# A fused memory-attention and squared-ReLU feed-forward kernel: scores copied out of PSUM at once, z pieces kept whole, weights converted two units at a time, and all batches in one pipeline of units

## The chip, the cores and the metric

The kernel runs on one core of one Trainium2 chip. The metric is the device time of one execution in microseconds (us). Three timed runs of the kernel before gave 759.39, 759.55 and 759.56 us, a median of 759.55 us. One more execution was taken with the hardware profiler on; all durations below come from it.

## What is computed

The reference, cut to what matters, with 8 batches (B), 8 heads (H), 512 tokens (S), 32 memory states (Ns) of 64 numbers each (D), a model width of 512 and a hidden width of 2048:

```python
scores = scale * np.matmul(x, state.transpose(0, 1, 3, 2))
scores = scores - scores.max(-1, keepdims=True)
a = np.exp(scores)
a /= a.sum(-1, keepdims=True) + 1e-09
xread = np.matmul(a, state)
scores2 = scale * np.matmul(state, x.transpose(0, 1, 3, 2))
...
sread = np.matmul(a2, x)
attn = np.concatenate([xread, sread], axis=2)
...
h = x @ w_in
r = np.maximum(h, 0.0)
return ((r * r) @ w_out).astype(np.float32)
```

The tokens read from the states (a softmax over 32 states), the states read from the tokens (a softmax over 512 tokens), and the 8 x (512 + 32) rows that come out go through a feed-forward layer with a squared ReLU. The weights arrive as 64-bit floating-point numbers, everything else as 32-bit ones.

## The kernel before, in words

**One unit of work.** The hidden width is cut into 16 slices of 128 (NFC). For one batch and one slice, a *unit* is `up` and `down` in `mlp` (L263 to L313). `up` makes `ph`, 128 hidden numbers by 512 tokens, in 6 matmuls; then a ReLU on ScalarE (`r`, L276), the square (ScalarE for the first 10 units, L278, VectorE for the rest, L280), and the split into a high and a low part (`g_hi` on ScalarE, L81; `g_lo` on VectorE, L82). `down` multiplies these by a slice of `w_out` into four PSUM tiles `po`, 12 matmuls (L300). `down` of a unit comes two `up`s later. Every precise product is done as three: high by high, low by high, high by low. There are 128 units for the tokens, and then 16 narrower ones for all 256 state rows together.

**z instead of xread.** The tokens' rows are never formed. Since xread is a times state, xread @ w_in is a @ (state @ w_in). The kernel makes z = state @ w_in for each batch in *pieces* of 1, 2 or 4 slices (`z_piece`, L110). A piece is 8 small matmuls (L130), each on a part of the array (64 rows by 32 columns), then a split into `z_hi` and `z_lo`.

**Attention.** `scores` makes `pst` (both score matrices at once, L167) in 8 such small matmuls. From `pst`, still in PSUM, VectorE makes a blockwise transposed copy `q1` for the softmax over states (`turn1`, L200), and then takes the maximum over tokens (`exps2`, L182), after which ScalarE reads `pst` again for the exponentials (L185). `soft1` and `soft1b` (L205 to L221) finish the softmax over the states and give `a_hi` and `a_lo`, which `up` needs. `turn` and `read` (L224 to L255) give the states' rows, `sr`. The tiles `pst`, `pz`, `pt` and `pr` all live in one PSUM buffer (`ps_x`, tag "px", one buffer), one after the other.

**Weights.** Each unit's slice of `w_in` and of `w_out` is loaded as 512 KB of doubles into one of 5 buffers (`load_w`, RAW = 5) and turned into singles by one ScalarE and three VectorE instructions (`singles`, L92 to L101). `w_out` is also split, the low part on GpSimd. All of this is done once, within the first 103 us, beside the first units.

**The order of the work.** The program is written as units in a row; between any two halves of a unit `aux` puts in what is due: conversions (`weights`), z pieces (`z_due`) and attention steps (`reads`), each queue by its due times. A scheduler then fixes the order on each engine by the order of writing, and moves an instruction ahead of others where it expects the engine to be idle. Each engine runs its own instructions strictly in that fixed order. The list BOTH sets how the first two batches take turns: batch 0 has units 0 to 7, batch 1 units 0 to 11, batch 0 the rest, batch 1 the rest; the other batches follow whole. Each such stretch is one call of `mlp` and ends with its own last two `down`s. The state rows go through another call at the very end.

## Time and profile before

| | |
|---|---|
| Median of 3 runs | 759.55 us (759.39 to 759.56) |
| The profiled execution's own time | 759.13 us |
| Its span in the profile, first to last instruction | 757.3 us |
| What lies outside the span | 1.83 us |
| TensorE (PE) busy | 687.0 us, 91% of the span |
| VectorE (DVE) busy | 399.4 us, 53% |
| ScalarE (ACT) busy | 282.1 us, 37% |
| GpSimd (POOL) busy | 44.3 us, 6% |
| Mean granted TensorE clock | 0.977 |

How to read it: PE is TensorE's matrix multiplies, PEld its weight loads. A line such as `327.67 0.79 PE L300 MATMUL po<-wo_hi,g_hi ... x1 [2.83 <-ACT g_hi L81]` says that at 327.67 us a matmul of line 300 began and took 0.79 us; before it the engine had been idle for 2.83 us, until ScalarE had written `g_hi` on line 81. Matmuls overlap, so the distance from one start to the next is what one costs. The kernel's small matmuls are shown twice each (16 in the trace for 8 written). "PEclk" is the share of the full clock that TensorE was granted.

### The profile page before, as it was taken

How to read it: one execution, taken by the hardware profiler on the slowest of the kernel's cores; microseconds unless marked ns; L12 is line 12 of the kernel's file. 1: busy time of each engine (PE TensorE's matmuls, PEld its weight loads, DVE VectorE, ACT ScalarE, POOL GpSimd, SP SyncE). 2: the span in 40 equal slices, each digit the busy share in tenths (PEclk: the TensorE clock that was granted, in tenths of full speed). 3: DMA queues.
4: the chain of work that ended last, by engine and by line, in shares of the span. 5: the costliest groups of instructions: out<-in, count | busy, mean ns of one | idle time of the engine just before them, and what ended most of it. 6: DMA issues, size and time to landing. Idle time of an engine off the chain costs nothing.

```text
span 757.3 us, 9704 instructions
## 1 busy us (share of the span) xinstructions
PE 687.0 (91%) x3896; PEld 504.7 (67%) x3896; DVE 399.4 (53%) x624; ACT 282.1 (37%) x479; POOL 44.3 (6%) x31
## 2 busy tenths in 40 slices
PE   1477979999969999989998999899998999999997
PEld 0145657777736777757775768577776776778896
DVE  5999953343566724483346433562447543334543
ACT  3566653232333523352334323242324333323442
POOL 0234310000010100010000100010001000000000
PEclk9999989999979999999999999999999999999999
DMA  9755500000333000310031001300020101000101
GB/s 343 260 167 164 187 1 0 1 3 6 112 111 96 20 1 1 112 57 4 1 112 56 4 0 57 112 1 0 20 92 1 57 0 57 1 0 1 57 1 28
DMA packets 16172, 43.60 MB, mean 58 GB/s; under 512 B 1536, under 2 KB 2560, under 8 KB 15104
## 3 DMA queue, kind: packets, MB, share of 16 engines
q1 hardware_dynamic: 15936, 42.74, 16.1%
q8 instruction: 30, 0.49, 0.3%
q10 hardware_dynamic: 192, 0.26, 0.1%
q14 instruction: 14, 0.11, 0.1%
HBM read 34.08 MB, written 8.91 MB: 57 GB/s over the span
## 4 chain that ended last, share of the span: by engine, by line
PE 77%; DVE 10%; issue 7%; ACT 2%; DMA 2%; POOL 0%; SPq 0%; ACTq 0%; POOLq 0%; DVEq 0%
PE po L300 46%; PE ph L274 23%; PE pz L130 6%; DMA wi_raw<-w_in 2%; DVE wof L97 1%; DVE wi L97 1%; DVE q L200 1%; DVE wi L101 1%; DVE m L207 1%; DVE nm L182 1%; PE pr L244 1%; DVE wof L101 1%; PE pst L167 1%; ACT g_hi L81 1%; PE pt L232 1%
## 5 line engine op out<-in xcount | busy, mean ns | idle before, releaser
L300 PE MATMUL po<-wo_hi,g_hi 128*128 128x512 f32 x544 | 224.3, 412 | 21.7 <-ACT g_hi L81 21.7
L300 PE MATMUL po<-wo_lo,g_hi 128*128 128x512 f32 x544 | 218.7, 402 | 0.0
L280 DVE TENSOR_TENSOR ph<-ph,r 128x512 f32<-128x512 f32 (+1 forms) x134 | 88.8, 666 | 196.6 <-ACT r L276 196.3
L276 ACT ACTIVATE r<-ph 128x512 f32<-128x512 f32 (+1 forms) x144 | 82.6, 575 | 261.8 <-PE ph L274 261.7
L300 PE MATMUL po<-wo_hi,g_lo 128*128 128x512 f32 x544 | 155.9, 396 | 0.0
L300 PEld LDWEIGHTS po<-wo_hi,g_hi 128*128 128x128 f32 x544 | 105.3, 194 | 73.2 <-ACT g_hi L81 37.0
L82 DVE TENSOR_TENSOR g_lo<-ph,g_hi 128x512 fp32r<-128x512 f32 (+1 forms) x144 | 94.9, 660 | 78.3 <-ACT g_hi L81 42.7
L300 PEld LDWEIGHTS po<-wo_lo,g_hi 128*128 128x128 f32 x544 | 105.5, 194 | 21.6
L300 PEld LDWEIGHTS po<-wo_hi,g_lo 128*128 128x128 f32 x544 | 101.4, 189 | 26.2 <-issue 5.0
L81 ACT CAST g_hi<-ph 128x512 fp32r<-128x512 f32 (+1 forms) x144 | 81.1, 564 | 91.2 <-DVE ph L280 63.0
L274 PE MATMUL ph<-a_hi,z_hi 128*128 128x512 f32 x256 | 84.5, 414 | 6.8 <-ACT a_hi L81 3.4
L274 PE MATMUL ph<-a_lo,z_hi 128*128 128x512 f32 x256 | 80.8, 398 | 1.8 <-DVE a_lo L82 1.8
L274 PE MATMUL ph<-a_hi,z_lo 128*128 128x512 f32 x256 | 82.2, 402 | 0.0
L130 PE MATMUL pz<-wi,sp_raw 64*32 64x512 f32 (+2 forms) x592 | 56.1, 583 | 25.6 <-ACT wo_hi L81 9.7
L274 PEld LDWEIGHTS ph<-a_hi,z_hi 128*128 128x128 f32 x256 | 47.0, 193 | 28.9 <-ACT a_hi L81 6.3
L274 PEld LDWEIGHTS ph<-a_hi,z_lo 128*128 128x128 f32 x256 | 49.1, 194 | 15.3 <-issue 4.2
L82 DVE TENSOR_TENSOR z_lo<-pz,z_hi 128x1024 fp32r<-128x1024 f32 (+2 forms) x39 | 39.9, 1028 | 35.8 <-ACT z_hi L81 35.8
L274 PEld LDWEIGHTS ph<-a_lo,z_hi 128*128 128x128 f32 x256 | 48.7, 191 | 13.6 <-DVE a_lo L82 2.5
L81 ACT CAST z_hi<-pz 128x1024 fp32r<-128x1024 f32 (+2 forms) x39 | 33.3, 860 | 39.4 <-PE pz L130 39.4
L82 POOL TENSOR_TENSOR a_lo<-at,a_hi 128x1024 fp32r<-128x1024 f32 x7 | 17.1, 2436 | 469.6 <-ACT a_hi L81 393.4
L130 PEld LDWEIGHTS pz<-wi,sp_raw 64*32 64x32 f32 x592 | 9.3, 110 | 47.4 <-issue 15.7
L82 POOL TENSOR_TENSOR wo_lo<-wof,wo_hi 128x512 fp32r<-128x512 f32 x16 | 22.5, 1406 | 65.6 <-ACT wo_hi L81 65.6
(61 smaller groups left out, 406.9 us busy)
## 6 DMA issues: line engine op xcount, KB each, us to landing
wi_raw<-w_in SPq DMA_DIRECT2D x16, 512.0 KB, 3.7
xt_raw<-xT SPq DMA_DIRECT2D x8, 1024.0 KB, 4.8
wo_raw<-w_out SPq DMA_DIRECT2D x16, 512.0 KB, 4.5
xn_raw<-xn SPq DMA_DIRECT2D x8, 1024.0 KB, 5.6
out<-sum SPq DMA_DIRECT2D x32, 256.0 KB, 2.3
sp_raw<-stP SPq DMA_DIRECT2D x8, 64.0 KB, 1.9
out<-os__5498 SPq DMA_DIRECT2D x2, 64.0 KB, 1.7
out<-os__5498 ACTq DMA_DIRECT2D x2, 64.0 KB, 2.0
```

The source lines that it names most:

```text
L81: nc.scalar.copy(out=hi, in_=src)
L82: eng_lo.tensor_sub(out=lo, in0=src, in1=hi.bitcast(F32))
L97: nc.vector.scalar_tensor_tensor(out=bits, in0=high, scalar=-0x80000000, in1=bits, op0=ALU.bitwise_and, op1=ALU.bitwise_or,)
L101: nc.vector.scalar_tensor_tensor(out=bits, in0=low, scalar=29, in1=bits, op0=ALU.logical_shift_right, op1=ALU.bitwise_or,)
L130: nc.tensor.matmul(pz[g][j * N:(j + 1) * N], lhsT=state[b][rows, j, :], rhs=wi[rows, j, cols], start=True, stop=True,)
L167: nc.tensor.matmul(pst[j * N:(j + 1) * N, g, :], lhsT=state[b][rows, j, :], rhs=my["t"][rows, j, :], start=True, stop=True,)
L182: nc.vector.tensor_reduce(out=nm2, in_=pst, axis=AX.X, op=ALU.max, negate=True)
L200: nc.vector.transpose(out=my["q1"][:, gs].rearrange("p g j n -> p (g j n)"), in_=my["pst"][:, gs].rearrange("p g s -> p (g s)"),)
L274: nc.tensor.matmul(ph, lhsT=w, rhs=v, start=i == 0, stop=i == len(todo) - 1)
L276: nc.scalar.activation(r, ph, AF.Relu)
L280: nc.vector.tensor_mul(out=ph, in0=ph, in1=r)
L300: nc.tensor.matmul(po[t], lhsT=g, rhs=w, start=i == 0 and j == 0, stop=i == last and j == 2)
```

## The change

Nothing changes in what is computed. The edits:

- **z pieces** are written under a raised priority (HURRY), so that the scheduler places a piece's 8 matmuls together and early.
- **Scores**: `scores` now ends with a ScalarE copy of `pst` into `e2`; the maximum and the exponentials of `exps2` read that copy, so `pst` is held only until that copy and `turn1` are done. `exps2` moves behind the other softmax in the order. For batch 0 the scores and the softmax over states are written under raised priority.
- **The states' read**: the eight scalings on VectorE become one multiply and four copies on GpSimd. The low parts of `w_out`, and batch 1's three softmax steps that were on GpSimd, go to VectorE.
- **Conversions** take two units at a time: 1 MB loads into 3 buffers, instructions twice as wide, one `wof` buffer instead of two. The first pair of `w_in` is loaded and converted in halves.
- **One pipeline**: `mlp` takes a list of all parts, the state rows as the last, and runs their units in one loop, so the last two `down`s of a part stand between the next part's `up`s. `r` has one buffer instead of two. The first 16 units square on ScalarE, not the first 10.
- **BOTH** becomes batch 0 units 0 to 3, batch 1 units 0 to 7, batch 0 the rest, batch 1 the rest. The attention of a batch may begin when the batch two before it has ended, so batch 2's may now begin 8 units before its own first unit, where it was 4.

```diff
-    RAW = 5
-    BOTH = ((0, 8), (1, 12), (0, NFC), (1, NFC))
+    RAW = 3
+    BOTH = ((0, 4), (1, 8), (0, NFC), (1, NFC))
...
+    HURRY = 120
...
         def run():
+            with tc.high_priority(offset=HURRY):
+                make()
...
+            nc.scalar.copy(out=my["e2"], in_=pst)
 
         def exps2():
-            pst, nm2 = my["pst"], my["nm2"]
-            nc.vector.tensor_reduce(out=nm2, in_=pst, axis=AX.X, op=ALU.max, negate=True)
+            e2, nm2, s2 = my["e2"], my["nm2"], my["s2"]
+            nc.vector.tensor_reduce(out=nm2, in_=e2, axis=AX.X, op=ALU.max, negate=True)
...
-                pool_for(b == 1).tensor_sub(out=q1, in0=q1, in1=wide(my["m1"]))
+                nc.vector.tensor_sub(out=q1, in0=q1, in1=wide(my["m1"]))
...
-                pool_for(b == 1).tensor_mul(out=q1, in0=q1, in1=wide(my["s1"]))
+                nc.vector.tensor_mul(out=q1, in0=q1, in1=wide(my["s1"]))
...
-                split(pair[0][:, gs], pair[1][:, gs], my["at"][:, gs], pool_for(b > 0))
+                split(pair[0][:, gs], pair[1][:, gs], my["at"][:, gs], (nc.gpsimd if b > 1 else nc.vector))
...
+            rd = sb.tile([P, NG, D], F32, name="rd", bufs=1)
+            nc.vector.tensor_mul(
+                out=rd, in0=pr[:, :, :D], in1=my["s2"].rearrange("p (g o) -> p g o", o=1)
...
-                    nc.vector.tensor_scalar_mul(
-                        sr[b // GB][at:at + N, c:c + D], pr[own, g, :D], my["s2"][own, g:g + 1]
-                    )
+                nc.gpsimd.tensor_copy(
...
-    def mlp(width, fcs, first, rows, aux):
+    def mlp(parts, aux):
...
-            r = sb.tile([P, S], F32, name="r", bufs=2)[:, :width]
+            r = sb.tile([P, S], F32, name="r", bufs=1)[:, :width]
             nc.scalar.activation(r, ph, AF.Relu)
-            if units[0] < 10:
+            if n < NFC:
...
-        for i in range(len(fcs) + 2):
-            if i <= last:
-                up(fcs[i])
+        for n in range(len(todo_) + 2):
+            if n < len(todo_):
+                up(n)
                 aux()
-            if i >= 2:
-                down(i - 2)
-            if i <= last:
+            if n >= 2:
+                down(n - 2)
+            if n < len(todo_):
                 aux()
...
-        raw = sb.tile([P, DM, 2], I32, name=f"{kind}_raw", tag="raw", bufs=RAW)
+        raw = sb.tile([P, 2 * DM, 2], I32, name=f"{kind}_raw", tag="raw", bufs=RAW)
...
-        wf = sb.tile([P, DM], F32, name="wof", bufs=2)
-        singles(wf, raw)
-        split(wo[0][:, fc, :], wo[1][:, fc, :], wf, nc.gpsimd)
+        wf = sb.tile([P, 2, DM], F32, name="wof", bufs=1)
+        singles(wf, raw.rearrange("p (u e) w -> p u e w", u=2))
+        split(wo[0][:, 2 * k:2 * k + 2, :], wo[1][:, 2 * k:2 * k + 2, :], wf, nc.vector)
...
-        return [w["pad"], w["load_t"], w["scores"], p[0], w["exps2"], p[1], p[2]]
+        return [w["pad"], w["load_t"], w["scores"], p[0], p[1], p[2], w["exps2"]]
...
-    mlp(NS, range(NFC), first, rows, lambda: None)
+    mlp([batch(*p) for p in parts] + [states()], aux)
```

What the instructions' fixed order shows of it, at three places. In these rows a name ending in a number is one buffer of that name, "x5" is the count of equal rows, and the line numbers are those of the kernel that the rows are from.

**First place: TensorE, inside a later batch.** The kernel before, where a z piece (`pz`) of 8 small matmuls stands among the large ones of `up` (`ph`) and `down` (`po`):

```order
L300 MATMUL po_2818<-wo_hi,g_lo 128x512
L130 MATMUL pz<-wi,sp_raw 32x512 x5
L274 MATMUL ph<-a_hi,z_hi 128x512 x2
L274 MATMUL ph<-a_hi,z_lo 128x512 x2
L274 MATMUL ph<-a_lo,z_hi 128x512 x2
L130 MATMUL pz<-wi,sp_raw 32x512
L300 MATMUL po_2815<-wo_hi,g_hi 128x512
```

The same engine in the changed kernel, at a piece of a later batch:

```order
L307 MATMUL po_1556<-wo_hi,g_lo 128x512
L132 MATMUL pz<-wi,sp_raw 32x512 x8
L307 MATMUL po_1553<-wo_hi,g_hi 128x512
L307 MATMUL po_1553<-wo_lo,g_hi 128x512
L307 MATMUL po_1554<-wo_hi,g_hi 128x512
```

The pieces that stood in two to four places now stand in one. Over the whole program the 37 pieces stood in 55 groups (2 of 128 columns, 10 of 256, 43 of 512) and now stand in 37 (2, 7 and 28). The scores `pst` go the other way: 8 groups before, 13 after (five of the eight are cut into 6 and 2). `pt` goes from 17 groups to 13, and `pr` from 8 to 13.

**Second place: TensorE, where the scores of batch 4 are made.** The kernel before, with `down` (`po`) finished for every unit whose `up` is done, and two `up`s open at once around the scores `pst`:

```order
L300 MATMUL po_2244<-wo_hi,g_lo 128x512
L274 MATMUL ph<-a_hi,z_hi 128x512 x4
L167 MATMUL pst<-xt_raw,sp_raw 32x512 x8
L274 MATMUL ph<-a_hi,z_lo 128x512 x2
L274 MATMUL ph<-a_lo,z_hi 128x512 x2
L274 MATMUL ph<-a_hi,z_lo 128x512 x2
L274 MATMUL ph<-a_lo,z_hi 128x512 x2
L300 MATMUL po_2241<-wo_hi,g_hi 128x512
```

The changed kernel at the scores of the same batch:

```order
L281 MATMUL ph<-a_lo,z_hi 128x512 x2
L169 MATMUL pst<-xt_raw,sp_raw 32x512 x6
L307 MATMUL po_2126<-wo_hi,g_hi 128x512
L307 MATMUL po_2126<-wo_lo,g_hi 128x512
L307 MATMUL po_2127<-wo_hi,g_hi 128x512
...
L307 MATMUL po_2129<-wo_hi,g_lo 128x512
L169 MATMUL pst<-xt_raw,sp_raw 32x512 x2
L281 MATMUL ph<-a_hi,z_hi 128x512 x2
L281 MATMUL ph<-a_hi,z_lo 128x512 x2
L281 MATMUL ph<-a_lo,z_hi 128x512 x2
L307 MATMUL po_2126<-wo_hi,g_hi 128x512
```

Before, the scores stood when 52 `down`s were done and two `up`s (53 and 54) were in the making; now they begin when 51 `up`s and 48 `down`s are done, so that three units' `down`s are still to come. For batch 2 the scores stood after 32 `up`s, its own first unit being number 33; now they stand after 27.

**Third place: VectorE, behind the eighth `g_lo`.** The kernel before; `wi` and `wof` are the slices of the two weights under conversion, `sum` is the output of the first part:

```order
L82 TENSOR_TENSOR g_lo<-ph,g_hi 128x512
L97 SCALAR_TENSOR_TENSOR wof<-wo_raw,wof 128x512
L101 SCALAR_TENSOR_TENSOR wi<-wi_raw,wi 128x4x128
L101 SCALAR_TENSOR_TENSOR wof<-wo_raw,wof 128x512
L93 TENSOR_SCALAR wof<-wof 128x512
...
L321 COPY sum<-po_324 128x512
L321 COPY sum<-po_326 128x512
...
L82 TENSOR_TENSOR z_lo<-pz,z_hi 128x1024
L82 TENSOR_TENSOR g_lo<-ph,g_hi 128x512 x2
```

The changed kernel from the same `g_lo`:

```order
L79 TENSOR_TENSOR g_lo<-ph,g_hi 128x512
L94 SCALAR_TENSOR_TENSOR wi<-wi_raw,wi 128x4x256
L79 TENSOR_TENSOR g_lo<-ph,g_hi 128x512
L79 TENSOR_TENSOR wo_lo<-wof,wo_hi 128x1024
L98 SCALAR_TENSOR_TENSOR wi<-wi_raw,wi 128x4x256
L90 TENSOR_SCALAR wof<-wof 128x1024
L79 TENSOR_TENSOR g_lo<-ph,g_hi 128x512
L94 SCALAR_TENSOR_TENSOR wof<-wo_raw,wof 128x1024
L98 SCALAR_TENSOR_TENSOR wof<-wo_raw,wof 128x1024
L79 TENSOR_TENSOR g_lo<-ph,g_hi 128x512
```

Before, 15 instructions, 12 of them conversions, stood between the eighth `g_lo` and the ninth. Now there is one, and then at most four up to the next.

More of the change, by code (lines that the diff above doesn't have):

```diff
@@ L284, in up, with down @@
             split(hi, lo, ph, nc.vector)
-            gs[fc] = hi, lo
-        def down(i):
-            fc = fcs[i]
-            hi, lo = gs.pop(fc)
+            gs[n] = hi, lo
+        def down(n):
+            p, i = todo_[n]
+            nt, last, po = p["width"] // P, len(p["fcs"]) - 1, p["po"]
+            hi, lo = gs.pop(n)
             if not po:
@@ L429, in memory_attention_then_relu2_ffn @@
         while i <= fcs[-1]:
-            new = at[i] == now + i - fcs[0]
             n = ZC
-            if new:
+            if at[i] == now + i - fcs[0]:
                 n = 1 if i < 2 else 2
-            cover = range(i, i + n)
-            pieces.append((now + i - fcs[0], b, cover))
+            pieces.append((now + i - fcs[0], b, range(i, i + n)))
             i += n
@@ L441, in z_due @@
             first, b, cover = pieces[0]
-            if slot[0] < 2 * (first - 2) or ("wi", cover[-1]) in queue[converted[0]:]:
+            if slot[0] < 2 * (first - 3) or cover[-1] not in ready:
                 break
@@ L448, in memory_attention_then_relu2_ffn @@
     for s_ in (
-        w["pad"], load_next, w["load_t"], *[load_next] * (RAW - 1), convert_next, z_due,
-        w["scores"], p[0], p[1], q[0], q[1], p[2], q[2], w["exps2"], convert_next, z_due,
+        w["pad"], load_next, w["load_t"], load_next, load_next, convert("wi", 0, early), z_due,
     ):
         emit(s_)
+    with tc.high_priority():
+        for s_ in (w["scores"], p[0], q[0], p[1], q[1], p[2], q[2]):
+            emit(s_)
+    for s_ in (convert("wi", 0, late), z_due, w["exps2"]):
+        emit(s_)
     weights, reads = Ahead(), Ahead()
-    for m in range(NFC):
-        weights.add([convert_next] * (2 if m + 2 < NFC else 1), 2 * at[m])
+    for k in range(NK):
+        steps = [convert("wi", k + 1)] if k + 1 < NK else []
+        weights.add(steps + [convert("wo", k)], 2 * at[2 * k])
     for b in range(1, B + LATE):
@@ L471, in memory_attention_then_relu2_ffn, with batch, first @@
     sums = {}
-    for b, fcs in parts:
-        while any(w[2] not in emitted for w in attentions[b][2]):
-            reads.next()
-        def first(fc, b=b):
+    def batch(b, fcs):
+        def first(fc):
+            while any(w[2] not in emitted for w in attentions[b][2]):
+                reads.next()
             c, i = divmod(fc, ZC)
@@ L497, in rows @@
                 )
-        mlp(S, fcs, first, rows, aux)
-    while reads.done < len(reads.steps):
-        reads.next()
-    NS = B * N
-    x2_hi = sb.tile([P, NCC, NS], F32R, name="x2_hi", tag="a_hi", bufs=2)
-    x2_lo = sb.tile([P, NCC, NS], F32R, name="x2_lo", tag="a_lo", bufs=2)
-    for i in range(NGB):
-        pt = ps_x.tile([P, NCC, P], F32, name="pt2", tag="px")
-        for cc in range(NCC):
-            nc.tensor.transpose(
-                out=pt[:, cc, :], in_=sr[i][:, cc * P:(cc + 1) * P], identity=ident
-            )
-        split(x2_hi[:, :, i * P:(i + 1) * P], x2_lo[:, :, i * P:(i + 1) * P], pt, nc.vector)
@@ L533, in memory_attention_then_relu2_ffn, with states, turn2, run @@
-    mlp(NS, range(NFC), first, rows, lambda: None)
+        return dict(width=S, fcs=fcs, first=first, rows=rows)
+    def states():
+        NS = B * N
+        x2 = []
+        def turn2(i):
+            def run():
+                if not x2:
+                    x2.extend(
+                        sb.tile([P, NCC, NS], F32R, name=n, tag=t, bufs=2)
+                        for n, t in (("x2_hi", "a_hi"), ("x2_lo", "a_lo"))
+                    )
+                own = slice(i * P, (i + 1) * P)
+                pt = ps_x.tile([P, NCC, P], F32, name="pt2", tag="px")
+                for cc in range(NCC):
+                    nc.tensor.transpose(
+                        out=pt[:, cc, :], in_=sr[i][:, cc * P:(cc + 1) * P], identity=ident
+                    )
+                split(x2[0][:, :, own], x2[1][:, :, own], pt, nc.vector)
+            return run
+        def first(fc):
+            while reads.done < len(reads.steps):
+                reads.next()
+            w_hi = sb.tile([P, NCC, P], F32R, name="wi_hi", tag="z_hi", bufs=2)
+            w_lo = sb.tile([P, NCC, P], F32R, name="wi_lo", tag="z_lo", bufs=2)
+            split(w_hi, w_lo, wi[:, :, fc * P:(fc + 1) * P], nc.vector)
+            return [
+                (w[:, cc, :], v[:, cc, :])
+                for w, v in ((w_hi, x2[0]), (w_lo, x2[0]), (w_hi, x2[1]))
+                for cc in range(NCC)
+            ]
+        def rows(t, po):
+            tile_ = sb.tile([P, DM], F32, name="os_", tag="raw", bufs=RAW)
+            move(t, tile_, po)
+            for i in range(GB):
+                at = (t * GB + i) * R + S
+                queue = nc.scalar if i % 2 else nc.sync
+                queue.dma_start(out=out[at:at + N, :], in_=tile_[i * N:(i + 1) * N, :])
+        reads.add([turn2(i) for i in range(NGB)], 2 * ends[B - 1] - 2, 2 * ends[B - 1] - 8)
+        return dict(width=NS, fcs=range(NFC), first=first, rows=rows)
```

122 lines of the change are left out of this document (61 added, 61 removed).

## The prediction

> **What bounds the kernel now.** I read the stretches of time first, then TensorE's waits, then the timelines around each wait. Each stretch gives its length, the busy time of PE, PEld, DVE, ACT and POOL, the granted clock, the DMA engines' share and GB/s:
>
> ```profile
> 0.00:25.00 25.00, 4.18 (x64) 1.14 (x64) 17.36 (x35) 10.93 (x22) 1.98 (x7) 1.00 0.90 333
> 25.00:50.00 25.00, 13.25 (x54) 7.10 (x55) 25.00 (x42) 13.61 (x25) 7.46 (x5) 1.00 0.61 202
> 50.00:75.00 25.00, 20.15 (x107) 14.26 (x106) 25.00 (x37) 14.92 (x25) 9.70 (x6) 0.99 0.50 167
> 75.00:100.00 25.00, 18.82 (x80) 13.12 (x80) 24.63 (x37) 17.73 (x32) 8.29 (x7) 0.91 0.44 147
> 125.00:150.00 25.00, 25.00 (x118) 18.06 (x118) 9.19 (x13) 7.53 (x12) 0.00 (x0) 1.00 0.00 1
> ```
>
> From 25 to 100 us VectorE is full and TensorE has holes; behind that TensorE is full, with holes at a few places. So in the start an edit is worth what it takes from VectorE or reorders there, and later what it takes from TensorE's own row of matmuls, or from its waits. Those waits from 100 us on (total, times, longest) are:
>
> ```profile
> PE po L300 <- ACT g_hi L81: 19.7, 9, 5.7
> PE pt L232 <- DVE z_lo L82: 4.2, 1, 4.2
> PE pz L130 <- ACT e L185: 2.8, 1, 2.8
> PE pt L232 <- DVE sr L253: 0.4, 1, 0.4
> ```
>
> With one of 0.3 us that a later row shows (at 223.36) they come to 27.4 us, the one that ends at 99.31 us counted with them. Four of the nine in the first row are alike. This is the one at the scores of batch 4, TensorE first, then VectorE:
>
> ```profile
> 324.21 0.62 PE L274 MATMUL ph<-a_lo,z_hi 128*128 128x512 f32 x2
> 327.67 0.79 PE L300 MATMUL po<-wo_hi,g_hi 128*128 128x512 f32 x1 [2.83 <-ACT g_hi L81]
> 331.06 1.09 PE L130 MATMUL pz<-wi,sp_raw 64*32 64x512 f32 x16
> ```
>
> ```profile
> 322.90 1.25 DVE L200 STREAM_TRANSPOSE q<-pst 128x1024 f32<-128x1024 f32 x1 [3.31 <-PE pst L167]
> 324.08 1.19 DVE L182 TENSOR_REDUCE nm<-pst 128x2 f32<-128x1024 f32 x1
> 325.19 1.20 DVE L207 TENSOR_REDUCE m<-q 128x32 f32<-128x1024 f32 x1
> 326.31 0.69 DVE L280 TENSOR_TENSOR ph<-ph,r 128x512 f32<-128x512 f32 x1
> ```
>
> All `down`s are done there, so TensorE has nothing until the two open units are squared, and the squares stand on VectorE behind three instructions on the scores.
>
> **Waits that go: 27.4 us.** In the changed order three units' `down`s are still to come when the scores begin. What six matmuls of `up` and twelve of `down` take, and a ScalarE pass over 1024 columns:
>
> ```profile
> 121.02 1.40 PE ph L274 x6
> 122.41 2.79 PE po L300 x12
> ```
>
> ```profile
> 317.32 1.02 ACT L81 CAST z_hi<-pz 128x1024 fp32r<-128x1024 f32 x1 [3.48 <-PE pz L130]
> ```
>
> Three `down`s are 8.4 us of cover. VectorE needs 3.4 us from the first of its three instructions to the square (322.90 to 326.31), and ScalarE's new copy of the scores adds about 1.0 us ahead of the second. So the four waits of 2.83 us go. The two waits of batch 2 (4.2 and 2.8 us) go since its scores now stand five units ahead of its first `up`. I count the small ones as gone as well, and add 2.5 us for new ones: their number is unknown, between nothing and what the old small ones come to, twice over.
>
> **Slow matmuls behind the waits: 10.3 us.** After a wait TensorE runs at half speed for a while:
>
> ```profile
> 92.53 1.05 PE L130 MATMUL pz<-wi,sp_raw 64*32 64x512 f32 x4
> 99.31 0.79 PE L300 MATMUL po<-wo_hi,g_hi 128*128 128x512 f32 x1 [5.72 <-ACT g_hi L81]
> 103.02 1.11 PE L130 MATMUL pz<-wi,sp_raw 64*32 64x256 f32 x16
> 215.01 1.96 PE L130 MATMUL pz<-wi,sp_raw 64*32 64x512 f32 x16 [2.82 <-ACT e L185]
> 223.36 1.22 PE L274 MATMUL ph<-a_hi,z_hi 128*128 128x512 f32 x2 [0.26 <-ACT a_hi L81]
> ```
>
> Eight `po` matmuls stand between 327.67 and 331.06: 3.39 us where eight warm ones take 8 x 0.23 = 1.85, so 1.5 us lost, four times: 6.0. Between 99.31 and 103.02 it is 1.8. At batch 2 the pieces take 1.96 for 1.09 and 1.22 for 0.62; with the transposes between them taken alike (1.0) that is 2.5. [...]
>
> **z pieces kept whole: 11.5 us.** A whole piece and a quarter of one, as the kernel before has them:
>
> ```profile
> 338.70 1.09 PE L130 MATMUL pz<-wi,sp_raw 64*32 64x512 f32 x16
> 339.72 0.50 PE L300 MATMUL po<-wo_hi,g_hi 128*128 128x512 f32 x1
> 348.23 1.05 PE L130 MATMUL pz<-wi,sp_raw 64*32 64x512 f32 x4
> 349.21 0.50 PE L300 MATMUL po<-wo_hi,g_hi 128*128 128x512 f32 x1
> ```
>
> From start to next start the whole takes 1.02 us and the quarter 0.98: splitting a piece doubles its price. The `po` behind takes 0.1 us longer than its neighbours, so a part costs 1.1. The order loses 15 parts of 512 columns and 3 of 256. One of them (92.53) stood in front of a wait and cost nothing: 14 x 1.1 = 15.4. For the narrow ones I take 0.7, between half and the whole: 2.1. Against that, the scores are cut in two five times: 5 x 1.1 = 5.5. `pt` and `pr` together gain one part, between nothing and 1.1; I take 0.5. Net 11.5. Its ends: 6 if a part costs 0.6, 13 if the scores' cut is free.
>
> **The start: nothing up to the eighth `g_lo`, then the wait of 5.72 us goes (counted above).** VectorE's instructions, their distances, and what GpSimd does to them:
>
> ```profile
> 79.22 1.22 DVE L82 TENSOR_TENSOR z_lo<-pz,z_hi 128x1024 fp32r<-128x1024 f32 x1
> 80.35 0.68 DVE L97 SCALAR_TENSOR_TENSOR wof<-wo_raw,wof 128x512 int32<-128x512 int32 x1
> 82.50 0.42 DVE L93 TENSOR_SCALAR wof<-wof 128x512 int32<-128x512 int32 x1
> 82.83 0.68 DVE L97 SCALAR_TENSOR_TENSOR wi<-wi_raw,wi 128x512 int32<-128x512 int32 x1
> 83.44 0.68 DVE L82 TENSOR_TENSOR g_lo<-ph,g_hi 128x512 fp32r<-128x512 f32 x1
> 87.74 0.68 DVE L82 TENSOR_TENSOR g_lo<-ph,g_hi 128x512 fp32r<-128x512 f32 x1
> 43.63 2.39 DVE L97 SCALAR_TENSOR_TENSOR wof<-wo_raw,wof 128x512 int32<-128x512 int32 x1
> ```
>
> ```profile
> 43.31 2.16 POOL L208 TENSOR_TENSOR q<-q,m 128x1024 f32<-128x1024 f32 x1
> ```
>
> Undisturbed distances are 1.13 us (79.22 to 80.35) for two inputs of 1024, 0.61 for 512, and 0.33 for a conversion's first step. At these, the order of before has 67.7 us of VectorE work up to the end of the eighth `g_lo`, which came at 88.4 (87.74 + 0.68). 7.6 us were idle (25.00 - 17.36 in the first stretch), so 13.1 us are stretching; the last two rows show it, a step of 0.68 us taking 2.39 beside a GpSimd subtraction.
>
> The changed order has 74.5 us up to there: 24 double conversion steps x 1.13, 13 first steps x 0.60 (no row has one at 1024; between 0.33 and 0.67), 6 single steps (3.1), 5 `wo_lo` that were on GpSimd (5.7), 8 `g_lo` (4.8), 19.8 for the two softmaxes, 3.4 of it from GpSimd, and 6.2 for the rest. GpSimd has nothing in this time, so no stretching. Waits come on top, since loads are now 1 MB:
>
> ```profile
> wi_raw<-w_in SPq DMA_DIRECT2D x16, 512.0 KB, 3.7
> xn_raw<-xn SPq DMA_DIRECT2D x8, 1024.0 KB, 5.6
> ```
>
> VectorE's second pair waits for 1 MB behind `xt`: some 2.4 us more idle, 10 in all. Later two loads are issued only as a buffer comes free, 5.6 us and a 1.0 us ScalarE step ahead of their use; ScalarE stands still for them with `r` and `g_hi` queued behind, and TensorE waits for those. Walking the order, I get 3 us there. 74.5 + 10 + 3 = 87.5, against 88.4 before: even. Ends: 81 with no waits, 97 if the last four loads each wait half their length more. Behind it, 12 conversion steps stood before the next `g_lo`; now at most four instructions, under 4.2 us, stand between two. That is what TensorE takes for a unit (1.40 + 2.79), so the wait goes.
>
> The remaining edits I cost at nothing: the states' read and the squares stand beside a TensorE that is full, VectorE being busy 9.19 of 25.00 us there; the narrow units' loop at the end has TensorE full already.
>
> **The sum.** 757.3 - 27.4 - 10.3 - 11.5 + 2.5 = 710.6 us of span. The profiled execution took 759.13, 1.83 outside the span, and the runs' median is 759.55, 0.4 more, which is within what I round: 712.
>
> **The rivals.**
>
> *The scores' waits stay.* VectorE still has two long instructions behind the scores ahead of a square, and ScalarE a copy. For it: the same instructions made the wait before. Against: 8.4 us of `down`s as cover. Price: 4 x (2.83 + 1.5) = 17.3, so 729.
>
> *The stretching is not GpSimd's doing.* Then VectorE, full already, gets 9.1 us of new work (5 `wo_lo`, three softmax steps) and keeps 13.1 us of stretching: the start ends 13 us later, at 725. Against it: 2.39 us beside a GpSimd instruction, 0.68 elsewhere. [...]
>
> *Slower: one `r` for two.* The ReLU of a unit may start only when the square of the one before has read `r`:
>
> ```profile
> L280 DVE TENSOR_TENSOR ph<-ph,r 128x512 f32<-128x512 f32 (+1 forms) x134 | 88.8, 666 | 196.6 <-ACT r L276 196.3
> L276 ACT ACTIVATE r<-ph 128x512 f32<-128x512 f32 (+1 forms) x144 | 82.6, 575 | 261.8 <-PE ph L274 261.7
> ```
>
> If that put half a microsecond into each of the 112 units squared on VectorE, 56 us would come: 768. It decides from (759 - 712) / 112 = 0.42 us a unit. Against: 0.58 + 0.67 us a unit of 4.2, and both engines wait 196 and 262 us for that very chain's input, so there is slack.
>
> **How the numbers follow.** The forecast 0.73, the scores' waits 0.11, the stretching 0.08, `r` 0.04; 0.02 that gains and losses cancel, 0.02 for better than the range. The range 702 to 728 holds the forecast with its ends (start 7 better, or 9 worse with the parts at 0.6) and the stretching rival. Differences up to 0.2% are what a measurement here can't tell from none. Faster 0.94, same 0.02, slower 0.04.
>
> **What would show it.** Right: TensorE's waits behind 100 us sum to a few us; no 2.83 us wait at scores; `pz` in 37 groups; the eighth `g_lo` near 88 us and TensorE without a hole of over 2 us behind it; no conversion step of over 1.3 us. Wrong: waits of `po` on `g_hi` after scores; the full stretch of VectorE reaching past 105 us; ReLUs that wait for VectorE.

## The result, and the profile after

The changed kernel takes **702.85 us** (median of 4 runs, 701.79 to 704.15) where the kernel before takes 759.47 (759.31 to 759.56): a ratio of 0.9255, 95% interval 0.9238 to 0.9273. The forecast was 712, in a range from 702 to 728. The profiled execution of the changed kernel took 703.47 us, with a span of 701.7.

The first row of each page says what kind of time went. Busy time, share of the span and instructions by engine, before:

```profile
PE 687.0 (91%) x3896; PEld 504.7 (67%) x3896; DVE 399.4 (53%) x624; ACT 282.1 (37%) x479; POOL 44.3 (6%) x31
```

and after:

```profile
PE 658.0 (94%) x3896; PEld 495.8 (71%) x3896; DVE 371.2 (53%) x528; ACT 289.2 (41%) x470; POOL 24.3 (3%) x44
```

TensorE runs the same 3896 instructions in 29.0 us less busy time, and it is idle 43.7 us (701.7 - 658.0) where it was idle 70.3 (757.3 - 687.0), 26.6 less. Together that is the whole difference of the spans, 55.6 us. So half of the gain is waiting that went, and half is the same matmuls taking less time.

**Waiting.** The stretches of time after, with the columns as before:

```profile
25.00:50.00 25.00, 14.86 (x79) 7.71 (x80) 25.00 (x36) 15.36 (x24) 0.00 (x0) 1.00 0.62 215
50.00:75.00 25.00, 17.69 (x93) 11.95 (x93) 23.02 (x30) 15.64 (x23) 0.00 (x0) 0.96 0.39 148
75.00:100.00 25.00, 25.00 (x120) 19.94 (x120) 22.85 (x25) 17.63 (x27) 0.00 (x0) 0.97 0.40 147
```

TensorE is full from 75 us on (it was busy for 18.82 of the 25 us from 75 to 100), and the list of waits has no row at all between 95 us and the end. The last wait of the program, from TensorE's timeline, with one ahead of it:

```profile
63.88 0.73 PE L281 MATMUL ph<-a_hi,z_hi 128*128 128x512 f32 x2 [2.36 <-ACT a_hi L78]
...
72.44 0.50 PE L307 MATMUL po<-wo_hi,g_hi 128*128 128x512 f32 x1 [3.25 <-ACT g_hi L78]
...
73.06 0.63 PE L307 MATMUL po<-wo_hi,g_hi 128*128 128x512 f32 x1
```

The scores of batch 4 after, TensorE:

```profile
356.72 1.08 PE L169 MATMUL pst<-xt_raw,sp_raw 64*32 64x512 f32 x12
357.72 0.50 PE L307 MATMUL po<-wo_hi,g_hi 128*128 128x512 f32 x1
...
360.68 1.05 PE L169 MATMUL pst<-xt_raw,sp_raw 64*32 64x512 f32 x4
361.66 0.72 PE L281 MATMUL ph<-a_hi,z_hi 128*128 128x512 f32 x2
...
363.15 0.39 PE L307 MATMUL po<-wo_hi,g_hi 128*128 128x512 f32 x1
...
365.89 0.39 PE L307 MATMUL po<-wo_hi,g_hi 128*128 128x512 f32 x1
```

and VectorE:

```profile
362.82 1.25 DVE L205 STREAM_TRANSPOSE q<-pst 128x1024 f32<-128x1024 f32 x1 [0.95 <-ACT e L181]
363.99 1.18 DVE L185 TENSOR_REDUCE nm<-e 128x2 f32<-128x1024 f32 x1
365.09 0.69 DVE L287 TENSOR_TENSOR ph<-ph,r 128x512 f32<-128x512 f32 x1
```

The square still stands behind two long instructions on the scores. But three `down`s (from 357.72, 363.15 and 365.89) are open when the scores begin, and TensorE is never out of work until the squared unit is ready.

**Busy time.** The small matmuls grouped by shape, with their total busy time and the mean of one in ns, before:

```profile
L130 PE MATMUL pz<-wi,sp_raw 64*32 64x512 f32 x448 | 46.9, 618 | 2.8 <-ACT e L185 2.8
...
L167 PE MATMUL pst<-xt_raw,sp_raw 64*32 64x512 f32 x128 | 10.5, 715 | 4.8 <-DVE z_lo L82 4.8
...
L130 PE MATMUL pz<-wi,sp_raw 64*32 64x256 f32 x112 | 7.8, 492 | 13.4 <-ACT wo_hi L81 9.7 <-ACT e L185 3.6
```

and after:

```profile
L132 PE MATMUL pz<-wi,sp_raw 64*32 64x512 f32 x448 | 31.4, 617 | 5.5 <-DVE z_lo L79 5.5
L169 PE MATMUL pst<-xt_raw,sp_raw 64*32 64x512 f32 x128 | 15.6, 715 | 8.0 <-DVE z_lo L79 5.9 <-DMA xt_raw<-xT 2.1
...
L132 PE MATMUL pz<-wi,sp_raw 64*32 64x256 f32 x112 | 5.1, 422 | 7.2 <-DVE wi L98 7.2
```

The wide z pieces give 15.5 us for 15 parts less, the scores take 5.1 us more for 5 parts more: about 1 us a part in both, with the same number of matmuls. The mean of one matmul (618 and 617 ns) does not show this price, only the total does.

**The start.** The low parts `g_lo` on VectorE, the eighth and ninth:

```profile
87.84 0.68 DVE L79 TENSOR_TENSOR g_lo<-ph,g_hi 128x512 fp32r<-128x512 f32 x1
...
89.57 0.68 DVE L79 TENSOR_TENSOR g_lo<-ph,g_hi 128x512 fp32r<-128x512 f32 x1
```

The eighth ends at 88.5 us, against 88.4 before and 87.5 forecast. The ninth follows after one conversion step, and TensorE does not wait. At 99.31 us before and at 91.40 after, TensorE has ended the same ten `up`s and eight `down`s, so the two traces can be cut there (the changed kernel has one z piece of 256 columns more behind it, 0.6 us). Length, TensorE's busy time, granted clock, before:

```profile
0.00:99.31 99.31, 55.71 (x301) 0.98 0.62 214
99.31:757.30 657.99, 631.26 (x3596) 0.98 0.10 34
```

and after:

```profile
0.00:91.40 91.40, 53.13 (x316) 0.98 0.62 229
91.40:701.70 610.30, 604.88 (x3581) 1.00 0.11 37
```

7.9 us of the gain lie in the start and 47.7 behind it, 26.4 of these in busy time and 21.3 in waits.

### The profile page after: what moved, and what is told of

It is laid out like the page before. It is cut to its first block, busy times and chain, and to the rows that moved or that the text cites. A ratio compares the mean times of both kernels' runs of the same rounds, so it can differ in the third digit from the quotient of the medians.

```text
span 701.7 us, 9604 instructions
## 1 busy us (share of the span) xinstructions
PE 658.0 (94%) x3896; PEld 495.8 (71%) x3896; DVE 371.2 (53%) x528; ACT 289.2 (41%) x470; POOL 24.3 (3%) x44
## 4 chain that ended last, share of the span: by engine, by line
PE 89%; DVE 7%; DMA 1%; issue 1%; ACT 1%; SPq 0%
PE po L307 53%; PE ph L281 28%; PE pz L132 4%; PE pst L169 2%; DMA wi_raw<-w_in 1%; PE pr L246 1%; PE pt L234 1%; DVE wi L94 1%; DVE wi L98 1%; DVE wof L94 1%; DVE wof L98 1%; DVE wo_lo L79 0%; DVE wi L90 0%; DVE z_lo L79 0%; DVE m L212 0%
## 5 line engine op out<-in xcount | busy, mean ns | idle before, releaser
L307 PE MATMUL po<-wo_hi,g_hi 128*128 128x512 f32 x544 | 217.5, 400 | 4.4 <-ACT g_hi L78 4.4
L307 PE MATMUL po<-wo_lo,g_hi 128*128 128x512 f32 x544 | 214.8, 395 | 0.0
L287 DVE TENSOR_TENSOR ph<-ph,r 128x512 f32<-128x512 f32 (+1 forms) x128 | 84.9, 663 | 149.6 <-ACT r L283 149.6
L78 ACT CAST g_hi<-ph 128x512 fp32r<-128x512 f32 (+1 forms) x144 | 81.2, 564 | 131.2 <-DVE ph L287 89.0
L307 PEld LDWEIGHTS po<-wo_hi,g_hi 128*128 128x128 f32 x544 | 102.4, 188 | 38.3 <-ACT g_hi L78 7.7
L307 PEld LDWEIGHTS po<-wo_lo,g_hi 128*128 128x128 f32 x544 | 102.7, 189 | 25.2 <-issue 4.2
L281 PE MATMUL ph<-a_hi,z_hi 128*128 128x512 f32 x256 | 84.3, 409 | 4.4 <-ACT a_hi L78 2.8
L281 PE MATMUL ph<-a_hi,z_lo 128*128 128x512 f32 x256 | 81.9, 398 | 0.0
L281 PE MATMUL ph<-a_lo,z_hi 128*128 128x512 f32 x256 | 79.5, 393 | 1.0 <-DVE a_lo L79 1.0
L281 PEld LDWEIGHTS ph<-a_hi,z_hi 128*128 128x128 f32 x256 | 46.9, 191 | 30.0 <-issue 7.5
L281 PEld LDWEIGHTS ph<-a_hi,z_lo 128*128 128x128 f32 x256 | 48.7, 190 | 14.8 <-issue 4.2
L281 PEld LDWEIGHTS ph<-a_lo,z_hi 128*128 128x128 f32 x256 | 48.6, 190 | 12.7 <-DVE a_lo L79 1.9
L132 PE MATMUL pz<-wi,sp_raw 64*32 64x512 f32 (+2 forms) x592 | 37.8, 570 | 20.5 <-DVE wi L98 15.0
L78 ACT CAST z_hi<-pz 128x1024 fp32r<-128x1024 f32 (+2 forms) x39 | 33.4, 863 | 52.0 <-PE ph L281 41.8
L132 PEld LDWEIGHTS pz<-wi,sp_raw 64*32 64x32 f32 x592 | 7.1, 109 | 35.0 <-issue 14.6
L169 PE MATMUL pst<-xt_raw,sp_raw 64*32 64x512 f32 x128 | 15.6, 715 | 8.0 <-DVE z_lo L79 5.9
L257 POOL COPY sr<-rd 32x128 f32<-32x128 f32 x32 | 9.2, 288 | 390.3 <-DVE rd L251 389.3
```

Source lines behind the costliest of these rows:

```text
L78: nc.scalar.copy(out=hi, in_=src)
L132: nc.tensor.matmul(pz[g][j * N:(j + 1) * N], lhsT=state[b][rows, j, :], rhs=wi[rows, j, cols], start=True, stop=True,)
L169: nc.tensor.matmul(pst[j * N:(j + 1) * N, g, :], lhsT=state[b][rows, j, :], rhs=my["t"][rows, j, :], start=True, stop=True,)
L257: nc.gpsimd.tensor_copy(out=sr[b // GB][at:at + N, j * NG * D:(j + 1) * NG * D], in_=rd[j * N:(j + 1) * N].rearrange("p g d -> p (g d)"),)
L281: nc.tensor.matmul(ph, lhsT=w, rhs=v, start=m == 0, stop=m == len(todo) - 1)
L287: nc.vector.tensor_mul(out=ph, in0=ph, in1=r)
```

## The experiments

Twelve kernels were run. Each is timed against the kernel before, whose median was 758.5 to 758.8 us in these runs. The changed kernel was not timed again beside them. The kernel before came out 0.6 to 1.0 us faster here than in the result's runs, so a difference of up to 1 us from the changed kernel says nothing. Only the edit is shown, a long one in part.

### One by one off the changed kernel

**e1: no raised priority for z pieces.**

```diff
-            with tc.high_priority(offset=HURRY):
-                make()
+            make()
```

> The changed kernel without the raised priority of the z pieces; nothing else differs. In its order the pieces of 512 columns fall into 41 groups where the changed kernel has 28, those of 256 into 9 where it has 7; in exchange the scores stand whole again (8 groups for 13), the states' read too (8 for 13). Theory (a part costs its own time of about 1.0 us and 0.2 us of restart in the matmul behind it, whatever its size): 13 x 1.2 + 2 x 0.8 - 5 x 1.2 - 5 x 0.35 = +9.5 us, 712, and no new waits of TensorE. Rival 1 (a part costs what its columns cost, the splitting is nearly free): within 2 us of 703. Rival 2 (the priority matters because pieces come in time): waits of TensorE for z behind 100 us, and more than 715.

Measured: 715.39 us, ratio 0.9424 (0.9410 to 0.9438), 12.5 us more than the changed kernel. The group of the wide pieces:

```profile
L131 PE MATMUL pz<-wi,sp_raw 64*32 64x512 f32 x448 | 44.9, 618 | 5.5 <-DVE z_lo L79 5.5
```

It is 13.5 us longer for 13 parts more. The profiled execution was the fastest of the four (713.77), with a span of 712.0 us, 10.3 more than the changed kernel's. Two waits behind 100 us come to 1.9 us. That leaves 8.4 us for parts in the trace, and 10.6 by the medians, where 9.5 were expected: the price of a part is right within about 1 us. Rival 1 (splitting is free) is out, and of rival 2 there are the 1.9 us.

**e2: loops apart.**

```diff
-    mlp([batch(*p) for p in parts] + [states()], aux)
+    for p in [batch(*p) for p in parts] + [states()]:
+        mlp([p], aux)
```

> The changed kernel with one loop of units for each part again, so that all downs of a part are done before the next part's first up; copy of the scores, order of the softmax steps, weights and priorities stay as changed. Theory (the three open downs are what covers the squares behind the scores): a wait of po on g_hi of about 2.8 us comes back at the scores of batches 4 to 7, with half-speed matmuls behind it, 4 x (2.8 + 1.5) = 17 us; the scores stand whole in this order (8 groups for 13), 6 us less: +11, 714. Rival (the copy, or the scores' earlier place, removed the waits, not the pipeline): no such waits, and 697 for the whole scores.

Measured: 698.77 us, ratio 0.9211 (0.9198 to 0.9225). The theory fell, the rival's 697 holds. TensorE has no wait behind 95 us. Its timeline at the scores of batch 4:

```profile
358.90 1.09 PE L169 MATMUL pst<-xt_raw,sp_raw 64*32 64x512 f32 x16
359.92 0.73 PE L283 MATMUL ph<-a_hi,z_hi 128*128 128x512 f32 x2
...
361.41 0.40 PE L310 MATMUL po<-wo_hi,g_hi 128*128 128x512 f32 x1
...
364.17 0.62 PE L283 MATMUL ph<-a_hi,z_hi 128*128 128x512 f32 x2
```

One `up` and one whole `down` are left behind the scores although the loops are apart. The scheduler had moved them there. That fits cover as what counts, as the prediction said, but the single pipeline is not what makes it. With the rest there, the pipeline even costs 4.1 us.

**e3: no copy of the scores.**

```diff
-            nc.scalar.copy(out=my["e2"], in_=pst)
...
-            nc.vector.tensor_reduce(out=nm2, in_=e2, axis=AX.X, op=ALU.max, negate=True)
+            nc.vector.tensor_reduce(out=nm2, in_=pst, axis=AX.X, op=ALU.max, negate=True)
...
-                    e2[:, g, :], e2[:, g, :], AF.Exp, bias=nm2[:, g:g + 1], scale=SCALE,
+                    e2[:, g, :], pst[:, g, :], AF.Exp, bias=nm2[:, g:g + 1], scale=SCALE,
```

> The changed kernel without ScalarE's copy of the scores: maximum and exponentials read them from PSUM, at the changed place behind the first softmax. TensorE's order differs only in that the z piece behind the scores stands one unit later. Theory (the copy does nothing for the time, the three downs cover the chain): within 2 us of 703, no wait of TensorE over 1 us behind 100 us. Rival (the copy is needed, since it frees the one PSUM buffer for the z piece behind): a wait of pz for the exponentials at each of 6 batches, as the 2.8 us that the kernel before had at batch 2, with 1 us of slow matmuls each: +15 to +23 us.

Measured: 702.84 us, ratio 0.9270 (0.9254 to 0.9285), one wait of 0.4 us behind 95 us. The copy, first in the change's own list, does nothing for the time when the rest is there.

**e4: GpSimd's old share back.**

```diff
-        split(wo[0][:, 2 * k:2 * k + 2, :], wo[1][:, 2 * k:2 * k + 2, :], wf, nc.vector)
+        split(wo[0][:, 2 * k:2 * k + 2, :], wo[1][:, 2 * k:2 * k + 2, :], wf, nc.gpsimd)
...
-                nc.vector.tensor_sub(out=q1, in0=q1, in1=wide(my["m1"]))
+                (nc.gpsimd if b == 1 else nc.vector).tensor_sub(out=q1, in0=q1, in1=wide(my["m1"]))
```

(and the same for the multiply and `a_lo` of batch 1)

> The changed kernel with GpSimd doing again what it did before: the five wo_lo subtractions of the start, now 1024 columns each and the later ones too, and two steps and a_lo of batch 1's softmax. VectorE gets rid of about 9 us of work ahead of the eighth g_lo. TensorE's order is the same. Theory (VectorE's steps stretch beside GpSimd's): steps of 1.13 us show 2 us and more while GpSimd works, 13 us of stretching for 9 us of relief, the eighth g_lo some 4 us later than 90.3 and the end at 707. Rival (the stretching is not GpSimd's doing): no stretching, the eighth g_lo at about 81 to 85 us, the end at 694 to 699.

Measured: 706.78 us, ratio 0.9317 (0.9301 to 0.9334), the time that the theory had. GpSimd's timeline:

```profile
39.98 2.81 POOL L79 TENSOR_TENSOR wo_lo<-wof,wo_hi 128x1024 fp32r<-128x1024 f32 x1 [10.74 <-ACT wo_hi L78]
47.94 2.29 POOL L213 TENSOR_TENSOR q<-q,m 128x1024 f32<-128x1024 f32 x1 [5.15 <-DVE m L212]
```

and VectorE's at the same moments:

```profile
40.48 2.86 DVE L79 TENSOR_TENSOR a_lo<-at,a_hi 128x512 fp32r<-128x512 f32 x1
...
48.38 2.40 DVE L90 TENSOR_SCALAR wi<-wi 128x1024 int32<-128x1024 int32 x1
```

Steps that take 0.68 us in the changed kernel take 2.86 and 2.40 here and end 0.55 us after GpSimd's. The relief of VectorE is lost again: the eighth `g_lo` starts at 89.51, 1.7 us later than in the changed kernel, where some 4 us were expected (the 90.3 in the expectation is the end of the ninth `g_lo`; the eighth ends at 88.5). All in all GpSimd's share costs 3.9 us here (706.78 against 702.85).

### Where the waits at the scores come from

e2 left the question what made the four waits of 2.83 us. TensorE before, ahead of the scores at 321.71:

```profile
316.12 1.09 PE L130 MATMUL pz<-wi,sp_raw 64*32 64x512 f32 x16
...
320.70 1.08 PE L274 MATMUL ph<-a_hi,z_hi 128*128 128x512 f32 x4
321.71 1.09 PE L167 MATMUL pst<-xt_raw,sp_raw 64*32 64x512 f32 x16
```

Two `up`s begin together at 320.70 (of the 4 records two belong to each), 4.6 us after the z piece that they read, and by then every `down` is used up. In the diff stands a line that the prediction passed over: a z piece is due at `2 * (first - 3)` where it was at `2 * (first - 2)`, one unit earlier. Four kernels test it.

**e5: the kernel before with one loop over all batches' parts.** `mlp` is that of the change; the calls:

```diff
-        mlp(S, fcs, first, rows, aux)
+        return dict(width=S, fcs=fcs, first=first, rows=rows)
+
+    mlp([batch(*p) for p in parts], aux)
```

> The kernel before with one thing of the change: one loop of units over all batches' parts, so that the next part's ups stand ahead of the last downs of the part before (the narrow units stay a loop of their own). Its order has two parts more of z pieces of 512 columns and one of 256. Theory of the prediction (the downs left over cover the squares behind the scores): the four waits of 2.8 us and the slow matmuls behind them go, 17 us less, 3 us more for parts: 745. New theory (the first z piece of a part comes so late that both ups and the scores pile up behind it with every down done, with or without the loop; the ups that wait for z are next in line behind the scores in this order too): the waits stay, 759 to 763.

Measured: 748.27 us, ratio 0.9869 (0.9843 to 0.9896). By the number the old theory looks right, by the trace it is wrong. All four waits at scores are there, as the one at batch 4:

```profile
307.40 1.09 PE L167 MATMUL pst<-xt_raw,sp_raw 64*32 64x512 f32 x16
...
313.36 0.79 PE L305 MATMUL po<-wo_hi,g_hi 128*128 128x512 f32 x1 [2.83 <-ACT g_hi L81]
313.95 0.63 PE L305 MATMUL po<-wo_lo,g_hi 128*128 128x512 f32 x1
```

What went is the wait of 5.72 us at 99 us and the two of batch 2 (nothing over 1.6 us is left there). The loop is good for those three, about 10 us, and does nothing for the waits at the later scores.

**e6: the kernel before with z pieces due one unit earlier.**

```diff
-            if slot[0] < 2 * (first - 2) or ("wi", cover[-1]) in queue[converted[0]:]:
+            if slot[0] < 2 * (first - 3) or ("wi", cover[-1]) in queue[converted[0]:]:
```

> The kernel before with one thing of the change, a line that the prediction passed over: a z piece is due three units ahead of its use and not two. Pieces of 512 columns fall into 38 groups (43 before), those of 256 into 9 (10), the transposes into 21 (17). New theory (the waits at the scores come from the late z piece): the four waits of 2.8 us go, 17 us less, and 5 x 1.2 + 0.8 - 0.8 = 6 us of parts: 735. Theory of the prediction (the loop of units is needed): the waits stay, 6 us of parts alone: 753.

Measured: 737.66 us, ratio 0.9731 (0.9714 to 0.9749), 20.8 us less where 23 were expected. TensorE's waits at 99 us and at batch 2, the scores of batch 5, and the one wait behind them:

```profile
99.10 0.80 PE L300 MATMUL po<-wo_hi,g_hi 128*128 128x512 f32 x1 [5.96 <-ACT g_hi L81]
...
223.16 1.22 PE L274 MATMUL ph<-a_hi,z_hi 128*128 128x512 f32 x2 [4.45 <-ACT a_hi L81]
...
399.55 1.09 PE L167 MATMUL pst<-xt_raw,sp_raw 64*32 64x512 f32 x16
...
419.84 0.50 PE L300 MATMUL po<-wo_hi,g_hi 128*128 128x512 f32 x1 [0.20 <-ACT g_hi L81]
```

It is the mirror of e5: the waits at the scores are gone, and the other three stay. The first two `up`s of a batch still begin together, but some 16 us behind the scores (at 415.73 here), when VectorE is through with them, and 0.20 us is what TensorE then waits. One number in one line was worth the four waits.

**e7: late z pieces, loops apart and no priority, in the changed kernel.** The edits of e1 and e2, and `first - 2` again.

> The changed kernel with three things undone at once: one loop of units for each part, z pieces due two units ahead, and no raised priority of z pieces; copy, order of the softmax steps, weights in pairs and GpSimd's part stay as changed. In its order the two ups and the scores stand together behind the first z piece, as before. Groups: z of 512 columns 38 (28 in the changed kernel), of 256 9 (7), scores 8 (13), read 11 (13). New theory (with z late and the loops apart, all downs are done when the scores come): waits of po on g_hi of 2 to 3 us at batches 4 to 7 and slow matmuls behind them, 17 us, and 10 x 1.2 + 2 x 0.8 - 5 x 1.2 - 0.7 = 7 us for parts: 727. Rival (the copy and the order of the softmax steps are what removed the waits): parts alone, 710.

Measured: 714.80 us, ratio 0.9429 (0.9410 to 0.9448): nearer the rival's 710 than 727. Two `up`s pile up around the scores at two batches only (2 and 4); there TensorE waits

```profile
304.43 0.51 PE L309 MATMUL po<-wo_hi,g_hi 128*128 128x512 f32 x1 [1.23 <-ACT g_hi L78]
```

and not 2.83 us: on VectorE the square now stands behind two instructions on the scores, not three, and a z piece of 1.1 us stands in the gap. At the other batches the scheduler found another order. So an early z piece is sufficient (e6), but not necessary. In the changed kernel these waits are shorter without it too, by the changed order of the softmax steps and by what the scheduler makes of it. How these two share it was not separated.

**e8: the kernel before with the raised priority of z pieces.** The edit of e1 the other way round.

> The kernel before with one thing of the change: the raised priority of z pieces. Pieces of 512 columns fall into 29 groups (43 before), those of 256 stay at 10, the read goes from 8 to 18 and the transposes from 17 to 10. In this order one up, not two, stands behind the scores. Theory (1.2 us a part of z, 0.35 a part of the read, 0.2 of the transposes; the waits at the scores depend on when z is due, not on its priority): 14 x 1.2 - 10 x 0.35 + 7 x 0.2 = 14.7 us less, 744, the waits of 2.8 us there. Rival (the priority alone brings z early enough): the waits go too, 727.

Measured: 715.08 us, ratio 0.9433 (0.9416 to 0.9451), far past the theory and at the rival's side. 43.4 of the change's 56.6 us come with these few lines. Behind 95 us TensorE's waits come to 5.5 us, this being one of the two longest:

```profile
208.16 0.73 PE L278 MATMUL ph<-a_hi,z_hi 128*128 128x512 f32 x2 [1.14 <-ACT a_hi L81]
```

Priority makes a piece whole, and it seems to make it early too: the first `up` behind it stands ahead of the scores in this order. By the prices of the prediction and of the expectation above it brings 14.7 us of parts, 22 us of waits (27.4 less 5.5) and 10.3 us of slow matmuls, 47 together.

### What else there was to gain

**e9: scores, transposes and read kept whole as well.** The three loops of matmuls in `scores`, `turn` and `read` each get

```diff
+            with tc.high_priority(offset=HURRY):
```

> The changed kernel with the raised priority of the z pieces given to the scores, the transposes and the states' read as well. Groups in its order: z 35 as in the changed kernel, scores 8 (13), read 8 (13), transposes 10 (13); the three open downs at the scores stay. Theory (1.2 us a part of the scores, 0.35 of the read, 0.2 of the transposes): 5 x 1.2 + 5 x 0.35 + 3 x 0.2 = 8.3 us less, 694.5, no waits of TensorE behind 100 us. Rival (what is kept whole keeps somebody else waiting: z pieces and scores share one buffer, so a step that jumps ahead pushes a unit back): waits of TensorE for z or scores, 700 to 703.

Measured: 695.88 us (695.18 to 696.66), ratio 0.9175 (0.9158 to 0.9192), no wait behind 95 us. That is 7.0 us less than the changed kernel, of 8.3 expected, and the best of all kernels run. What the change took with one hand in z pieces it gave back with the other in scores; it did not have to.

**e10: weights one unit at a time.** Loads of 512 KB into six buffers, conversion steps of 512 columns, as in the kernel before; `wo_lo` stays on VectorE. Of the edit, the lines that set the order of the conversions:

```diff
-        steps = [convert("wi", k + 1)] if k + 1 < NK else []
-        weights.add(steps + [convert("wo", k)], 2 * at[2 * k])
+        weights.add([convert_next] * (2 if m + 2 < NFC else 1), 2 * at[m])
```

> The changed kernel with the weights loaded and converted one unit at a time, in 512 KB transfers and steps of 512 columns with six buffers of half the size; wo_lo stays on VectorE, all else as changed, and the groups of TensorE's order are the same. Theory of the prediction (a pair saves VectorE some 2 to 3 us of work in the start and costs 3 to 5 us of waits for 1 MB): 0 to 3 us faster than the changed kernel, 700 to 703, with fewer waits of VectorE for its data in the first 75 us. Rival (the pairs are a part of the gain: fewer and longer steps on a full VectorE): 705 to 708.

Measured: 714.60 us, ratio 0.9425 (0.9406 to 0.9444), 11.8 us more than the changed kernel: both expectations too low, the rival's sign right. VectorE has less idle time in the first 25 us (17.28 busy against 14.76), so the waits for 1 MB are real. But in the fixed order the softmax of batch 1 begins late. VectorE in this kernel:

```profile
46.83 1.24 DVE L205 STREAM_TRANSPOSE q<-pst 128x1024 f32<-128x1024 f32 x1
...
95.87 0.69 DVE L79 TENSOR_TENSOR g_lo<-ph,g_hi 128x512 fp32r<-128x512 f32 x1
```

and the same transpose in the changed kernel:

```profile
40.90 1.24 DVE L205 STREAM_TRANSPOSE q<-pst 128x1024 f32<-128x1024 f32 x1
```

Up to that transpose VectorE has ended 14 units' conversions here (last steps counted, `wi` and `wo`), 10 in the changed kernel. The eighth `g_lo` comes 8.0 us later, TensorE waits longer and then runs slow (mean granted clock 0.84 and 0.81 in the stretches from 50 to 75 and from 75 to 100 us, 0.96 and 0.97 in the changed kernel). VectorE's work up to 125 us is the same (97.7 us, 98.1 in the changed kernel), so the pairs do not pay by cheaper instructions. What the full engine does first is the likely reason, but it is not shown: the same order with single units was not tried.

**e11: the old turns of the first two batches.**

```diff
-    BOTH = ((0, 4), (1, 8), (0, NFC), (1, NFC))
+    BOTH = ((0, 8), (1, 12), (0, NFC), (1, NFC))
```

> The changed kernel with the parts of the first two batches as before (eight units of batch 0 and twelve of batch 1 first, where the change has four and eight). Scores, transposes and read are in 12 groups each (13). Theory (the waits at batch 2 went with the early z pieces, as they did in the kernel before with the priority alone, and the start is bound by VectorE's conversions, which the parts do not change): no wait over 1.5 us behind 100 us, 701 to 705. Rival (the parts put batch 2's scores far enough ahead, and more units of work per weight in the start): the waits of 4.2 and 2.8 us of batch 2 with slow matmuls, 9.5 us, and a later start: 712 or more.

Measured: 705.53 us, ratio 0.9299 (0.9281 to 0.9317), 2.7 us more than the changed kernel. The time is near the theory's, the trace near the rival's:

```profile
198.76 1.22 PE L281 MATMUL ph<-a_hi,z_hi 128*128 128x512 f32 x2 [6.92 <-ACT a_hi L78]
```

The wait of batch 2 is back, with slow matmuls behind it, and is paid for by a better start: TensorE is busy all of the time from 50 to 75 us, where it was busy 17.69 us in the changed kernel, and the eighth `g_lo` starts at 80.37.

**e12: the kernel before with one `r`.**

```diff
-            r = sb.tile([P, S], F32, name="r", bufs=2)[:, :width]
+            r = sb.tile([P, S], F32, name="r", bufs=1)[:, :width]
```

> The kernel before with one buffer r and not two, as the change has it. Theory (the chain of ReLU and square has slack): within 1.5 us of the kernel before. Rival of the prediction (a unit's ReLU waits for the square of the unit before, half a microsecond in each of 112 units): up to 56 us more, 815, and ReLUs that wait for VectorE in every unit.

Measured: 761.91 us, ratio 1.0045 (1.0029 to 1.0061), 3.2 us more, where the theory allowed 1.5. The ReLUs wait for TensorE alone:

```profile
L276 ACT ACTIVATE r<-ph 128x512 f32<-128x512 f32 (+1 forms) x144 | 82.6, 574 | 267.7 <-PE ph L274 267.5
```

The slower rival is out. The 3.2 us fit the order: the scheduler cut the wide z pieces into 48 groups here, 43 before, and their busy time is 51.2 us, 4.3 more.

## Why the prediction was right, point by point

- **Waits that go, 27.4 us, and 2.5 us of new ones.** All went, and no new one came behind 95 us: the 2.5 us are one part of the miss. The reason given, `down`s left over as cover, is what the timelines show. What puts them there is another matter. The prediction took the order as it is and did not ask which edit makes it. The runs say: at the scores, z pieces made early, by their due time (e6) or their priority (e8), and to a part the softmax steps' new order (e7); at 99 us and at batch 2, the priority (e8) or the loop (e5). For batch 2 the prediction named the scores' place ahead of the first `up`; e11 shows it in the changed kernel, where the old turns bring 6.92 us back. Most of these waits have two removers each, which is why undoing one edit (e1, e2, e3) brings none of them back.
- **Slow matmuls behind the waits, 10.3 us.** Behind 100 us they are there behind each wait of 2.83 us or more in e5 and e11 (0.63 us for a `po` of 0.39 in e5, 1.05 for a `ph` pair of 0.62 in e11), and gone where the wait is gone (granted clock 1.00 from 76.34 to 701 us in the changed kernel). The size was too low. Behind 99.31 us the prediction counted up to 103.02, but the next `up` is slow as well (0.62 us for such a pair elsewhere):

  ```profile
  104.05 1.22 PE L274 MATMUL ph<-a_hi,z_hi 128*128 128x512 f32 x2
  ```

  In the kernel before the granted clock is 0.50 from 98.51 to 105.34 us, from 214.57 to 224.81, and for 3.41 us at each of the four later waits. TensorE is busy 24.1 us in these stretches, so half of that is lost: 12.1 us, 1.8 more than forecast.
- **z pieces kept whole, 11.5 us.** The small matmuls' rows give 15.5 + 2.7 - 5.1, and `pt` and `pr` in the same view 1.5 and -1.0: 13.6 us. Of that, 0.9 for the piece at batch 2, 1.0 for the transposes and 0.4 for the piece at 103.02 are slow matmuls, which leaves 11.3. e1 (13.5 us for 13 parts) and e9 (7.0 us for 13 parts of three kinds) bear the price out. One end of this term is a slip: 13 "if the scores' cut is free" should be 11.5 + 5.5 = 17.0, so the better end of the range lies 4 us too high by the prediction's own numbers.
- **The start: even, then 5.72 us.** The eighth `g_lo` came at 88.5 against 87.5 in the forecast, and the wait behind it went. TensorE is through the tenth `up` and the eighth `down` at 91.4 us where the forecast gives 99.31 - 5.72 = 93.6: 2.2 us of the miss. VectorE's sum was right (75.6 us busy up to there, 74.5 forecast), but reading the start as a sum was too simple: e10 moves the eighth `g_lo` by 8.0 us to later and e11 by 7.5 to earlier, with VectorE's work up to 125 us within 0.6 us of the changed kernel's 98.1. GpSimd as the cause of the stretching is confirmed (e4).
- **The sum.** Forecast span 710.6, measured 701.7: 8.9 us better. Cut as above, 2.2 lie in the start. Behind it 47.7 us went where the sum has 21.7 + 10.3 + 11.5 - 2.5 = 41.0. Of these 6.7 us, 2.1 are waits (21.3 against 21.7 - 2.5) and 4.6 busy time (26.4 against 21.8). Of the busy time, 0.6 is the z piece that the changed kernel already has behind it at the cut, and 1.8 are the slow matmuls. The other term that was mis-sized is "a part costs 1.1": beside its own time a part costs 0.11 us in the first large matmul behind it (0.50 for 0.39, at 357.72) and some 0.1 us in front of it, and only the first was counted. TensorE's order has 71 stretches of small matmuls where it had 83, so that is 12 x 0.1 = 1.2 us. The remaining 1.0 us has no cause that a run shows. All these errors point the same way, and 702.85 is 0.85 us from the end of the range: the mechanisms were right, but that the time still lies inside the range is in part luck.
- **The rivals.** The scores' waits did not stay, the stretching was GpSimd's (e4), and one `r` makes no ReLU wait for VectorE (e12). What the list lacked is a question of another kind: how much one edit brings alone. By e8 the z pieces' priority brings 43.4 us of the 56.6.

## What to carry to other kernels

Where an order written by a scheduler changes, price the order that comes out, as was done here; but before saying which edit is to thank, look for each due time and priority in the diff, and undo one and add one. Waits that have two removers do not show when one edit is undone, only when one is added alone (e8, e6, e5). And a time that fits a theory is not yet its proof: e5 and e11 both came within a few us of a theory that their traces contradict.
